# Attention read and soft mixture of experts in one kernel: twelve identity transposes ahead of the first load, and the first states moved from ACT's queue to SP's

## The chip, the cores and the metric

The kernel runs on one core of a Trainium2 chip. A core has five engines that each work through their own instructions in order: PE (TensorE, matrix products and transposes), DVE (VectorE), ACT (ScalarE), POOL (GpSimd) and SP (SyncE, which here only issues DMA transfers). PE loads its weights by separate instructions, shown as PEld. Transfers run on 16 DMA engines, whichever engine issued them. The metric is the device time of one execution in microseconds (us).

## The reference

Inputs: `x` of 8 batches, 8 heads, 512 tokens and 64 channels; `state` of 8 batches, 8 heads, 32 states and 64 channels; all f32.

```python
def _attn_ref(x, state):
    scores = scale * np.matmul(x, state.transpose(0, 1, 3, 2))
    a = softmax(scores)                     # over the 32 states
    xread = np.matmul(a, state)
    scores2 = scale * np.matmul(state, x.transpose(0, 1, 3, 2))
    a2 = softmax(scores2)                   # over the 512 tokens
    sread = np.matmul(a2, x)
    return np.concatenate([xread, sread], axis=2)

def _moe_ref(x, phi, w1, w2):               # x: 4608 rows (8 batches x 544) of 512
    logits = x @ phi                        # 32 slots = 8 experts x 4
    d = softmax over the rows of logits
    slot_input = d.T @ x
    for e in range(E):
        h = np.maximum(slot_input[e] @ w1[e], 0.0)
        slot_out[e] = h @ w2[e]
    c = softmax over the slots of logits
    return c @ slot_out
```

The softmaxes are written out in the reference with the maximum subtracted and 1e-9 added to the sum; `w1` is 8 x 512 x 1024, `w2` is 8 x 1024 x 512.

## The kernel before

The kernel has two stages. The first computes attention for batch 0 to 7 and gathers what the experts read. The second multiplies with `w1` (into `h_ps`), with `w2` (into `so_ps`), and writes the output.

The first stage is a list of small steps, `ORDER`, which is executed in the order in which it is written; each step issues a few instructions, and each engine then works through its own in that order. Steps that matter here, `b` the batch, `g` one of the four parts of a batch of `x` (two heads each), `h` one of two halves:

- `X.b.g` (PE, L203): four transposes of 128x128 of a part of `x` against the identity `ident`, into a PSUM buffer of the pool `ps_t`, which has three buffers that are used in turn.
- `xe.b.g` (ACT, L208): copies that buffer to SBUF as `xt` (times 0.125), which frees it.
- `S.b` (PE, L217): the scores `sc` of a batch, from its four `xt` and from its states `stT_sb`.
- `q`, `m1`, `m2` (DVE, L230, L235, L266): transposes the scores and takes maxima. `sub` (POOL, L239) subtracts, `x1` (ACT, L242) takes the exponential, `l1` (DVE, L246) sums.
- `G.0` (PE, L186) multiplies the states by `phi_bd`. `phi_bd` is a copy of the loaded `phi_sb` that POOL makes (L180). It is issued ahead of the whole list, so it stands before the first `sub` in POOL's order.

Batch 0 of `x` is loaded in four parts of 256 KB, 128 partitions by 512 elements, the others in two transfers of 512 KB. The states of batches 0 and 1 come as one transfer (128 KB, `stT_sb[:, 0:1]`, called the first states below), those of the other six as another (384 KB, the other states). In the kernel before, ACT issues the first states and then parts 1 and 3; SP issues parts 0 and 2, batch 1, the other states, `phi_sb`, batches 2 to 7, and then the weights. The transfers take eight semaphores in turn, and a transfer that reuses one waits on its issuing engine until the one eight places earlier has landed.

```python
    act.dma_start(stT_sb[:, 0:1], stT[:, 0:1])
...
            if b == 0:
                for g, eng in enumerate((nc.sync, act)):
                    eng.dma_start(t[:, g], xv[:, 2 * k + g])
            else:
                nc.sync.dma_start(t, xv[:, 2 * k : 2 * k + 2])
```

`ident` is made by POOL at the start (a memset and a select, masks.py). The buffers `big` hold `x`, states and weights; a weight is loaded when a buffer is free (`load_w`), in the second stage after each step of `w1_part` (L639) and `w2_part` (L699).

Of the kernel before, what the change touches and what calls it, by code (L numbers as in the profile page):

```python
# [8 lines left out]
F32 = mybir.dt.float32  # L9
# [6 lines left out]
P = 128  # L16
B = 8
S = 512
# [46 lines left out]
def attention_soft_moe(ctx: ExitStack, tc: tile.TileContext, x, stT, phi, w1, w2, out_x, out_s):  # L65
# [6 lines left out]
    nc = tc.nc  # L72
    pe, act, dve, pool = nc.tensor, nc.scalar, nc.vector, nc.gpsimd
# [5 lines left out]

    stT_sb = big.tile([P, 4, 2, 2, 2, NS], F32, tag="big", name="stT_sb")  # L80
    phi_sb = cp.tile([P, 4, NS], F32, name="phi_sb")
    act.dma_start(stT_sb[:, 0:1], stT[:, 0:1])
    xb = []
    for b in range(B):
        for k in range(2):
            t = big.tile([P, 2, NJ, 2 * D], F32, tag="big", name=f"x{b}_{k}")
            xv = x[b].rearrange("p (g j c) -> p g j c", g=4, j=NJ)
# [3 lines that stand above are left out]
            else:  # L91
                nc.sync.dma_start(t, xv[:, 2 * k : 2 * k + 2])
            xb.append(t)
        if b == 1:
            nc.sync.dma_start(stT_sb[:, 1:4], stT[:, 1:4])
            nc.sync.dma_start(phi_sb, phi)
# [29 lines left out]
    ident = cp.tile([P, P], F32, name="ident")  # L126
# [27 lines left out]
    with ExitStack() as actx:  # L154
# [3 lines left out]
        ps_t = actx.enter_context(tc.tile_pool(name="ps_t", bufs=3, space=PSUM))  # L158
# [13 lines left out]

        def mtile(shape, name):
            return ps_m.tile(shape, F32, tag="ms", name=name)


        phi_bd = wk.tile([P, 4, 2, NS], F32, tag="h", name="phi_bd", bufs=NH)
# [126 lines left out]
        def R_(b, h):  # L304
            r = R[b]
            if h == 0:
                r["srp"] = mtile([P, 2, D], f"sr_ps{b}")
            for j in range(NJ):
                for g in range(4):
                    pe.matmul(  # L310
                        r["srp"][32 * g : 32 * g + 32, h, :],
                        r[f"eT{h}"][:, j, 32 * g : 32 * g + 32],
                        xb[2 * b + g // 2][:, g % 2, j, D * h : D * h + D],
                        start=(j == 0),
                        stop=(j == NJ - 1),
                    )
            if h == 1:
                load_w(2)
# [6 lines left out]
        def srT(b):  # L325
            r = R[b]
            r["srTp"] = mtile([P, P], f"srT_ps{b}")
            pe.transpose(r["srTp"], r["sr"].rearrange("p h d -> p (h d)"), ident)
# [8 lines left out]
        def Lx(b, h):  # L337
            q, i = group(b)
            if h == 0 and i == 0:
                q["lt"] = mtile([P, len(q["b"]), P], f"lt_{b}")  # L340
            for j in range(NJ):
                pe.matmul(
                    q["lt"][32 * j : 32 * j + 32, i, :],
                    G_sb[:, b, h, :],
                    R[b][f"aT{h}"][:, P * j : P * j + P],
                    start=(h == 0),
                    stop=(h == 1),
                )
# [486 lines left out]
```

## Time and profile before

| | us |
|---|---|
| median of 3 runs | 137.98 (137.72 to 139.47) |
| profiled execution, its own time | 137.19 |
| span of the profiled execution, first to last instruction | 135.4 |
| PE busy | 115.8 (86% of the span) |
| DVE busy | 85.9 (63%) |
| ACT busy | 79.0 (58%) |
| POOL busy | 44.8 (33%) |
| DMA, mean rate | 382 GB/s, 51.76 MB |

The page cuts the span into 40 slices of 3.4 us and gives the busy share of each engine in tenths. In its groups, a row reads: line, engine, operation, output <- input, sizes, count. The timeline gives start, duration and count, and in brackets the idle time ahead and what ended it; SPq and ACTq are the DMA instructions on those engines' queues. Lists of transfers give the size and the time from issue to landing. The row of granted clock on the page stands at full speed from the start, so how fast PE runs is read from the durations of equal instructions.

### The profile page before, as it was taken

The page shows a single profiled execution, that of the slowest core. Times are in us where ns is not written, and L with a number is a line of the kernel's source. Part 1 is how long each engine was busy: PE and PEld are TensorE (multiplying, and loading weights), DVE is VectorE, ACT ScalarE, POOL GpSimd, SP SyncE. Part 2 cuts the span into 40 slices and gives each one's busy share as a digit, 9 for nine tenths or more (in the row PEclk, how much of TensorE's full clock was granted, in tenths as well). Part 3 has the DMA queues.
Part 4 walks back from the last instruction along what each step waited for, and adds up shares of the span by engine and source line. Part 5 has one row for each costly group of instructions (what it writes and reads, how often), then busy time and mean ns, then how long its engine had stood idle before and what let it go on. Part 6 is the DMA issues. An engine that isn't in the chain of part 4 may idle for free.

```text
span 135.4 us, 5043 instructions
## 1 busy us (share of the span) xinstructions
PE 115.8 (86%) x2103; PEld 81.8 (60%) x2103; DVE 85.9 (63%) x216; ACT 79.0 (58%) x195; POOL 44.8 (33%) x64
## 2 busy tenths in 40 slices
PE   0479899999999999999989968999997999999500
PEld 0354667869597875757766748962596458493100
DVE  2002999999999999999998359209930361524700
ACT  3042999999999998897994920410101371625600
POOL 3001635376375535338778163402500000000000
PEclk9999999999999999999999999999999999999955
DMA  3999999999999999999999952999999999999992
GB/s 86 307 408 421 421 414 420 413 418 420 415 410 421 412 422 413 419 414 424 412 413 418 416 236 62 407 415 418 419 420 412 422 404 413 413 413 377 420 416 92
DMA packets 14854, 51.76 MB, mean 382 GB/s; under 512 B 1648, under 2 KB 1904, under 8 KB 14832
## 3 DMA queue, kind: packets, MB, share of 16 engines
q1 hardware_dynamic: 14400, 50.80, 93.4%
q10 hardware_dynamic: 432, 0.66, 1.4%
q8 instruction: 16, 0.26, 0.7%
q14 instruction: 6, 0.05, 0.1%
HBM read 42.53 MB, written 8.91 MB: 380 GB/s over the span
## 4 chain that ended last, share of the span: by engine, by line
DVE 41%; PE 37%; ACT 7%; issue 4%; DMA 4%; DVEq 1%; ACTq 0%
PE so_ps L699 11%; PE h_ps L639 11%; DVE l1s L246 7%; PE o L729 7%; DVE aT L260 6%; DVE q L230 6%; DVE nm L266 6%; DVE m L235 5%; DMA x<-x_in 4%; DVE r L251 3%; ACT xt L208 2%; PE xt_ps L203 2%; PE sc L217 2%; PE os L747 2%; DVE r L250 1%
## 5 line engine op out<-in xcount | busy, mean ns | idle before, releaser
L203 PE MATMUL xt_ps<-ident,x 128*128 128x128 f32 x128 | 20.1, 296 | 6.1 <-DMA x<-x_in 5.3
L208 ACT ACTIVATE xt<-xt_ps 128x512 f32<-128x512 f32 x32 | 18.8, 617 | 7.6 <-PE xt_ps L203 7.6
L239 POOL TENSOR_TENSOR q<-q,m 128x512 f32<-128x512 f32 x16 | 16.7, 1049 | 19.0 <-DVE m L235 11.9
L739 DVE COPY out<-o 128x512 f32<-128x512 f32 x16 | 10.3, 686 | 18.6 <-PE o L729 18.6
L203 PEld LDWEIGHTS xt_ps<-ident,x 128*128 128x128 f32 x128 | 15.4, 151 | 9.6 <-issue 5.7
L255 POOL TENSOR_TENSOR q<-q,r 128x512 f32<-128x512 f32 x16 | 16.7, 1049 | 8.0 <-DVE r L251 2.7
L230 DVE STREAM_TRANSPOSE q<-sc 128x512 f32<-128x512 f32 x16 | 11.1, 695 | 10.3 <-PE sc L217 10.3
L699 PEld LDWEIGHTS so_ps<-w,h_m 128*32 128x32 f32 x512 | 13.8, 110 | 4.2 <-issue 4.1
L699 PE MATMUL so_ps<-w,h_m 128*32 128x128 f32 x512 | 15.6, 274 | 0.7 <-issue 0.7
L639 PE MATMUL h_ps<-w,si_m 128*32 128x512 f32 x128 | 14.4, 594 | 0.4 <-DVE si_m L611 0.4
L738 ACT COPY out<-o 128x512 f32<-128x512 f32 x16 | 8.6, 588 | 7.2 <-PE o L729 7.2
L271 ACT ACTIVATE e<-sc,nm 128x512 f32<-128x512 f32 x16 | 11.2, 706 | 1.2 <-DVE q L230 0.4
L639 PEld LDWEIGHTS h_ps<-w,si_m 128*32 128x32 f32 x128 | 9.1, 110 | 4.2 <-issue 2.9
L260 DVE STREAM_TRANSPOSE aT<-q 128x512 f32<-128x512 f32 x16 | 10.6, 684 | 0.0
L246 DVE TENSOR_REDUCE l1s<-q 128x16 f32<-128x512 f32 x16 | 10.5, 657 | 0.0
L310 PE MATMUL sr_ps<-x,eT 128*32 128x64 f32 x512 | 10.3, 220 | 0.3 <-ACT eT L293 0.3
L242 ACT ACTIVATE q<-q 128x512 f32<-128x512 f32 x16 | 10.5, 658 | 0.0
L266 DVE TENSOR_REDUCE nm<-sc 128x1 f32<-128x512 f32 x16 | 10.5, 660 | 0.0
L235 DVE TENSOR_REDUCE m<-q 128x16 f32<-128x512 f32 x16 | 10.5, 659 | 0.0
L285 PE MATMUL eT_ps<-ident,e 128*128 128x128 f32 x64 | 10.0, 279 | 0.5 <-ACT e L271 0.5
L217 PE MATMUL sc<-xt,stT_sb 64*32 64x512 f32 x128 | 10.2, 653 | 0.0
L285 PE MATMUL an_ps<-ident,aT 128*128 128x128 f32 x64 | 9.9, 280 | 0.2 <-DVE aT L260 0.2
(115 smaller groups left out, 179.5 us busy)
## 6 DMA issues: line engine op xcount, KB each, us to landing
w<-w_in SPq DMA_DIRECT2D x64, 512.0 KB, 10.0
out_x<-out SPq DMA_DIRECT2D x16, 512.0 KB, 6.4
x<-x_in SPq DMA_DIRECT2D x14, 512.0 KB, 8.3
x<-x_in SPq DMA_DIRECT2D x2, 256.0 KB, 4.0
x<-x_in ACTq DMA_DIRECT2D x2, 256.0 KB, 6.2
out_s<-out_s SPq DMA_DIRECT2D x2, 256.0 KB, 5.9
stT_sb<-stT_in SPq DMA_DIRECT2D x1, 384.0 KB, 8.2
stT_sb<-stT_in ACTq DMA_DIRECT2D x1, 128.0 KB, 3.7
```

The costliest lines, as they stand in the source:

```text
L203: pe.transpose(p[:, P * j : P * j + P], xb[2 * b + g // 2][:, g % 2, j, :], ident)
L208: act.mul(r[f"xt{g}"], r[f"xp{g}"], 0.125)
L230: dve.transpose(r[f"q{h}"], r[f"sp{h}"])
L235: dve.tensor_reduce(out=r[f"m1{h}"], in_=r[f"qv{h}"], axis=AX.X, op=ALU.max)
L239: pool.tensor_tensor(v, v, R[b][f"m1{h}"].broadcast_to([P, 16, NS]), op=ALU.subtract)
L246: dve.tensor_reduce(out=l1s[:, i, :, 0:1], in_=R[b][f"qv{h}"], axis=AX.X, op=ALU.add)
L255: pool.tensor_tensor(v, v, R[b][f"r1{h}"].broadcast_to([P, 16, NS]), op=ALU.mult)
L260: dve.transpose(r[f"aT{h}"], r[f"q{h}"])
L266: dve.tensor_reduce(out=r[f"nm2{h}"], in_=r[f"sp{h}"], axis=AX.X, op=ALU.max, negate=True)
L285: pe.transpose(p[:, j, :], r[f"{src}{h}"][:, P * j : P * j + P], ident)
L639: pe.matmul(h_ps[hf][32 * kt : 32 * kt + 32, :], si_m[kt // 2][:, 256 * (kt % 2) + 32 * e : 256 * (kt % 2) + 32 * e + 32], w1t[hf, e, kt], ...
L699: pe.matmul(so[k][32 * i : 32 * i + 32, :], h_m[hf][:, 256 * i + 32 * e : 256 * i + 32 * e + 32], w2t[k, e, 4 * hf + i], start=(hf == 0 an ...
```

## The change

The first states leave ACT's queue and are issued by SP behind parts 0 and 2 of batch 0. ACT issues parts 1 and 3 alone. PE gets twelve transposes of the identity against itself into a buffer `spin` of the pool `ps_t`, ahead of the first step; nothing reads them.

```diff
     stT_sb = big.tile([P, 4, 2, 2, 2, NS], F32, tag="big", name="stT_sb")
     phi_sb = cp.tile([P, 4, NS], F32, name="phi_sb")
-    act.dma_start(stT_sb[:, 0:1], stT[:, 0:1])
     xb = []
...
             xb.append(t)
+        if b == 0:
+            nc.sync.dma_start(stT_sb[:, 0:1], stT[:, 0:1])
         if b == 1:
             nc.sync.dma_start(stT_sb[:, 1:4], stT[:, 1:4])
             nc.sync.dma_start(phi_sb, phi)
...
             return ps_m.tile(shape, F32, tag="ms", name=name)
+
+
+        spin = ps_t.tile([P, S], F32, tag="tr", name="spin")
+        for i in range(12):
+            pe.transpose(spin[:, P * (i % 4) : P * (i % 4) + P], ident, ident)
```

The rows below are the first of each engine, in its own order; lines are those of the two kernels (L90, L92 before are L89, L91 after; L203 is L209; L217 is L223). Names carry a running number at their end; `x_0` is the tile of parts 0 and 1 of a batch, `x_1` that of parts 2 and 3. First ACT at the start of the program, before and then after:

```order
L82 DMA stT_sb<-stT_in 128x256
L90 DMA x_0_66<-x_in 128x512
L90 DMA x_1_69<-x_in 128x512
L208 ACT_TABLE_LOAD
L208 ACTIVATE xt_1_211<-xt_ps_1_201 128x512
```

```order
L89 DMA x_0_65<-x_in 128x512
L89 DMA x_1_68<-x_in 128x512
L214 ACT_TABLE_LOAD
L214 ACTIVATE xt_1_224<-xt_ps_1_214 128x512
L214 ACTIVATE xt_0_226<-xt_ps_0_209 128x512
```

Parts 1 and 3 each move up by one place. The copies behind them keep their order (part 1 before part 0). Now SP at the start, before and then after:

```order
L90 DMA x_0_66<-x_in 128x512
L90 DMA x_1_69<-x_in 128x512
L92 DMA x_0_72<-x_in 128x1024
L92 DMA x_1_74<-x_in 128x1024
L95 DMA stT_sb<-stT_in 128x768
L96 DMA phi_sb<-phi_in 128x128
L92 DMA x_0_78<-x_in 128x1024
```

```order
L89 DMA x_0_65<-x_in 128x512
L89 DMA x_1_68<-x_in 128x512
L94 DMA stT_sb<-stT_in 128x256
L91 DMA x_0_72<-x_in 128x1024
L91 DMA x_1_74<-x_in 128x1024
L96 DMA stT_sb<-stT_in 128x768
L97 DMA phi_sb<-phi_in 128x128
L91 DMA x_0_78<-x_in 128x1024
```

The first states stand third on SP; batch 1, the other states and `phi_sb` each move down by one. Before, `phi_sb` waited on SP for the first states to land; now it waits for part 1. Last PE at the start, after the change:

```order
L180 MATMUL spin<-ident 128x128 x12
L209 MATMUL xt_ps_0_209<-ident,x_0_65 128x128 x4
L209 MATMUL xt_ps_1_214<-ident,x_0_65 128x128 x4
L209 MATMUL xt_ps_2_219<-ident,x_1_68 128x128 x4
L209 MATMUL xt_ps_3_230<-ident,x_1_68 128x128 x4
L223 MATMUL sc_0_237<-xt_0_226,stT_sb 32x512
```

The twelve transposes are the only new rows on PE. `spin` takes the first buffer of `ps_t`, so each later tile of that pool sits one buffer further on; the fourth part's buffer still comes free with the copy of part 0, as before. DVE's and POOL's rows are as they were.

## The prediction, made before the changed kernel ran

> **What bounds the kernel now.** I read the stretches of time first. Columns: start:end, length, busy time and count of PE, PEld, DVE, ACT and POOL, granted clock, DMA share, GB/s.
>
> ```profile
> 20.00:40.00 20.00, 19.70 (x378) 15.59 (x379) 19.78 (x47) 19.68 (x48) 11.49 (x12) 1.00 1.03 416
> 40.00:60.00 20.00, 19.25 (x391) 14.09 (x389) 19.65 (x54) 18.92 (x51) 8.61 (x10) 1.00 1.03 417
> 79.00:85.00 6.00, 4.48 (x59) 3.89 (x55) 5.17 (x16) 0.62 (x1) 3.17 (x4) 1.00 0.37 122
> 85.00:95.00 10.00, 10.00 (x94) 6.13 (x89) 3.79 (x12) 1.59 (x4) 2.31 (x3) 1.00 1.03 417
> ```
>
> In the middle of the first stage DVE works 19.78 of 20 us, so this stage ends as much earlier as DVE's stream starts earlier, if nothing else holds it. The DMA engines run full (1.03) around one hole, 79 to 85 us, where the second stage has not yet freed buffers. Then the start, in the chain of waits (start, us, what):
>
> ```profile
> 1.17 5.13 DMA x<-x_in
> ...
> 6.34 1.13 PE xt_ps L203 x4
> ...
> 7.49 1.58 ACT xt L208 x3
> ...
> 9.12 1.09 PE xt_ps L203 x4
> 10.21 2.35 PE sc L217 x16
> ```
>
> DVE's first work on scores starts when `S.0` ends (12.55). Ahead of that stand a late part 1, the transposes, ACT's copies, the transposes of part 3, and 2.4 us of scores. Equal PE instructions are slower here than later (line, engine, operation, count, ns min/median/max, first and last start):
>
> ```profile
> L203 PE MATMUL xt_ps<-ident,x x12: 421/421/476, 4.3 to 7.9; 128*128 128x128 f32 x12
> L203 PE MATMUL xt_ps<-ident,x x16: 272/273/330, 12.5 to 14.2; 128*128 128x128 f32 x16
> L217 PE MATMUL sc<-xt,stT_sb x16: 801/1056/1060, 10.1 to 11.8; 64*32 64x512 f32 x16
> L217 PE MATMUL sc<-xt,stT_sb x16: 589/601/613, 17.2 to 17.8; 64*32 64x512 f32 x16
> ```
>
> PE runs at about 57% speed until the last scores of `S.0` (801 lies between 1056 and 601, so it changes near 12.3), and fast from then on.
>
> **The change, part by part.** All sums are made against the profiled execution: 137.19 us of its own, span 135.4, so 1.8 lie around the span. It is 0.8 under the median of 137.98.
>
> *The twelve transposes.* The identity's select, and PE's blocks in the timeline (start, us, ..., idle before and what ended it):
>
> ```profile
> 1.01 0.29 POOL masks.py:199 TENSOR_SCALAR_AFFINE_SELECT ident<-ident 128x128 f32<-128x128 f32 x1
> 6.34 1.97 PE L203 MATMUL xt_ps<-ident,x 128*128 128x128 f32 x8 [0.91 <-DMA x<-x_in]
> 12.48 2.00 PE L203 MATMUL xt_ps<-ident,x 128*128 128x128 f32 x16
> 17.19 1.18 PE L217 MATMUL sc<-xt,stT_sb 64*32 64x512 f32 x16
> ```
>
> At the early speed, transposes follow each other every (1.97 - 0.42)/7 = 0.22 us, at the later speed every (2.00 - 0.27)/15 = 0.115. Twelve from 1.35 at the early speed take 11 x 0.22 + 0.42 = 2.84 and end at 4.2, when part 0 lands (below): they cost nothing, being in idle time. What they may bring is an earlier fast PE. Before, 1.97 us of unbroken work (6.34 to 8.31) did not make it fast; the unbroken stretch from 9.12 to 12.3, 3.2 us, did. Work from 1.35 on, followed without a break over 0.2 us by slow parts 0 and 1, gives fast PE at 4.6 at the earliest. I take 6, and 8 as the late bound.
>
> The Trainium skill, page "TensorE: Matmul & The Clock Gate", part 1 ("The HAM clock gate"), says that activity is judged in windows of 3.4 us that run freely, not from the kernel's start. The 3.2 us above agree with a window; by that rule PE's full speed comes at 4.8 to 8.2, anywhere between from run to run, which my bounds already span. The same part calls the slow phase's penalty under 1% of a typical span: by that alone the time would not fall under 135.8. The rows of the chain speak against using it so, since here the slow stretch stands ahead of everything that DVE does.
>
> *The loads.* First issues, then size and time from issue to landing:
>
> ```profile
> 0.73 0.41 ACTq L82 DMA_DIRECT2D stT_sb<-stT_in  x1
> 0.74 0.85 SPq L90 DMA_DIRECT2D x<-x_in  x2
> 1.17 0.94 ACTq L90 DMA_DIRECT2D x<-x_in  x2
> ...
> stT_sb<-stT_in ACTq DMA_DIRECT2D x1, 128.0 KB, 3.7
> x<-x_in SPq DMA_DIRECT2D x1, 256.0 KB, 3.5
> x<-x_in SPq DMA_DIRECT2D x1, 256.0 KB, 4.5
> x<-x_in ACTq DMA_DIRECT2D x1, 256.0 KB, 5.1
> x<-x_in ACTq DMA_DIRECT2D x1, 256.0 KB, 7.3
> ```
>
> So part 0 lands at 4.24, the first states at 4.43, part 2 (issued at 1.16) at 5.7, part 1 at 6.3, part 3 (issued at 1.64) at 8.9. SP's batch 1, issued from 1.64 on, runs beside parts 1 and 3 and delays them. Counted by landings, 384 KB are there at 4.43 and 896 at 6.3. After the change parts 0 and 1 share the engines first: 512 KB at 4.43 + 1.87 x 128/512 = 4.9. At the same 0.47 us for each 128 KB, parts 2 and 3 make 1024 KB at 6.8, and the first states 1152 KB at 7.2. These are estimates from the landings above. Bounds for part 3: 5.7, where SP's second 256 KB landed, and 8.9, as now. I take 6.8.
>
> The same skill's page "DMA: Bandwidth & Descriptors" ("Issuing engines are not separate DMA queues") says that all issuers share the 16 engines and a second issuer saves only issue time. By that alone part 3 would land 0.4 us earlier, at 8.5, its transposes with it, which is rival 4 below. The trace has 7.3 us for 256 KB on ACT beside 4.5 on SP, issued half a microsecond apart, so which queue carries what did matter for landing.
>
> *`S.0` after the change.* Parts 0 and 1 are transposed by 6.0 (fast) to 6.9 (slow, 1.97 from 4.9). ACT then copies part 1 and part 0, some 0.55 each (1.58 for three): the buffer of part 3 is free at 7.1 to 8.0, later than the part lands. Its transposes take 0.66, its copy 0.6, and the last scores end some 0.7 after: 9.1 to 10.0. That is 2.55 to 3.45 earlier than 12.55; I take 3.0. The first states (7.2) are there before `S.0` begins.
>
> *What is late next.* The rows of POOL, ACT and DVE after `S.0`, and `phi_sb`:
>
> ```profile
> 4.42 0.33 SPq L96 DMA_DIRECT2D phi_sb<-phi_in  x1
> ...
> phi_sb<-phi_in SPq DMA_DIRECT2D x1, 64.0 KB, 6.5
> ...
> 11.08 0.62 POOL L180 COPY phi_bd<-phi_sb 64x128 f32<-64x128 f32 x2 [9.34 <-DMA phi_sb<-phi_in]
> 14.62 1.05 POOL L239 TENSOR_TENSOR q<-q,m 128x512 f32<-128x512 f32 x1 [2.93 <-DVE m L235]
> ...
> 15.76 0.66 ACT L242 ACTIVATE q<-q 128x512 f32<-128x512 f32 x1
> ...
> 16.45 0.69 DVE L246 TENSOR_REDUCE l1s<-q 128x16 f32<-128x512 f32 x1
> ```
>
> `phi_sb` lands at 10.92 and POOL copies until 11.70. `sub.0.0` stands behind these copies in POOL's order and has 2.9 us to spare now. The change does not bring `phi_sb` earlier: the bytes ahead of it on both queues are the same 2560 KB, and the 0.5 us later issue (it waits for part 1, 4.9, no longer for the states, 4.4) still finds SP's queue full. So `sub.0.0` starts at 11.72 at the earliest, `x1.0.0` at 12.86, and DVE's `l1.0.0` at 13.55: **2.9 us earlier and no more**, and all that DVE does later follows. This cap and the 3.0 of `S.0` lie close; with both of them I take 2.8 for the first stage (2.5 to 3.2; the upper end if `phi_sb` lands 0.3 earlier).
>
> *Does it reach the end?* Loads and outputs fill the DMA engines from 85 us to the end, so the second stage ends earlier only if they restart earlier. The hole of 79 to 85 us holds 6 x (1.03 - 0.37) = 4.0 us of transfers, more than 2.8. But single engines lag (here the columns are length, granted clock, DMA share, GB/s):
>
> ```profile
> 81.50:82.00 0.50, 1.00 0.08 33
> 82.00:82.50 0.50, 1.00 0.00 0
> ...
> 83.00:83.50 0.50, 1.00 0.00 0
> 83.50:84.00 0.50, 1.00 0.71 90
> ...
> 131.50:132.00 0.50, 0.50 1.03 422
> ...
> 133.00:133.50 0.50, 0.50 0.18 74
> ```
>
> A few engines still move the last weights until 82.0, and the second stage's first transfers start at 83.5. Restarting 2.8 earlier, at 80.7, they find the slowest still busy for 1.3 us. At the end of the kernel, too, the engines run full until 132 and the slowest until nearly 134. If these are not the same engines, a lag of 1.3 ends within those 2 us and costs nothing, which I take. If they are, only the 1.5 us of 82.0 to 83.5 are won.
>
> **Sum:** 0 (twelve transposes) - 2.8 (first stage) + 0 (hole) = -2.8; 137.19 - 2.8 = **134.4**.
>
> **The rivals.**
>
> 1. *A DMA engine that lags in both places takes part of the gain.* Only 1.5 us (2.0 at most, with the lag before 82) reach the end: 135.7, or 135.2. For it: full DMA engines from 85 us on. Against: nothing shows the engine to be the same.
> 2. *The clock does not come up with the twelve transposes.* Identity work may count for little, or a pause at 4.2 may reset it. Then parts 0 to 2 end at 7.9 and the scores follow slowly: from the start of part 3's transposes to the end of `S.0` it took 12.55 - 9.12 = 3.43, so 8.0 + 3.43 = 11.4, 1.1 earlier: 136.1. Against it: PE would have worked for over 6 us. The skill's bound of 1% on the slow phase, cited above, would end near here too, at 135.8 or more.
> 3. *`phi_sb` is no cap.* If it lands early, the early bound of `S.0` counts, 3.45: 133.7.
> 4. *Part 3 gains only ACT's earlier issue.* It lands at 8.97 - 0.44 = 8.5 (1.17 to 0.73 in the issues). With PE fast by then, transposes of 0.66, a copy of 0.6 and 0.7 for the last scores end `S.0` at 10.4 to 10.5, 2.1 earlier: 135.1. This is the same as what the skill's rule on issuers would give. Against it: SP's own 256 KB landed in 4.5.
> 5. *Slower: the first states come late on SP's queue.* They gate all of `S.0`. With PE fast it decides from a landing at 12.55 - 1.18 = 11.4. If they took 11.4 us from their issue at 1.6, as the slowest transfer of `x` did:
>
> ```profile
> DMA to landing us min/median/max: 3.5/7.7/11.4
> ```
>
> they would land at 13.0 and `S.0` would end at 14.2, 1.65 later: 138.8. Against it: SP's third transfer of now, four times as large, landed 6.8 us after issue.
>
> ```profile
> x<-x_in SPq DMA_DIRECT2D x1, 512.0 KB, 6.8
> ```
>
> **How the numbers follow.** Forecast 0.55, rival 1 0.15, rival 2 0.12, rival 3 0.08, rival 4 0.07, rival 5 0.03. The range 133.5 to 135.8 covers the forecast with its bounds (2.5 to 3.2, so 134.0 to 134.7) and rivals 1, 3 and 4, and leaves out 2 and 5. Two per cent, about what a measurement of this kernel tells from no change, is 135.2 from the median: under it lie the forecast, rival 3, rival 4 and a little of rival 1, 0.71. Within 2% lie the rest of rival 1, rival 2 and most of rival 5: 0.28. Slower by over 2%: 0.01.
>
> **What would show it.** In the profile after: twelve transposes from 1.35 to about 4.2; scores of `S.0` near 600 ns, ending at 9.1 to 10.0; part 3 landing near 6.8; POOL idle until `phi_sb` at about 11, then `sub.0.0` right behind its copies; `l1.0.0` at 13.5 instead of 16.45; the first products with `w1` 2.8 earlier than now; the DMA hole shrunk to about 1 us. I am wrong if the scores of `S.0` still take 1056 ns, if `l1.0.0` comes far from 13.5, or if the first stage ends 2.8 earlier and the kernel does not.

## The result, and the profile after

The changed kernel takes 134.2 us (median of 4 executions, 134.10 to 136.28) against 137.85 before (median of 4, 137.31 to 139.47). The ratio is 0.9746 with a 95% interval of 0.9707 to 0.9784: 2.5% faster. The profiled execution took 134.10 us, its span is 132.3. Executions more than 1.5% above the fastest of the same kernel (136.28 and 139.47 here) are left out of the ratio.

First the timeline of the changed kernel at its start: start, us, engine, line, operation, count, and the idle time ahead with what ended it.

```profile
1.36 2.82 PE L180 MATMUL spin<-ident 128*128 128x128 f32 x12 [1.36 <-POOL ident masks.py:199]
4.66 2.17 PE L209 MATMUL xt_ps<-ident,x 128*128 128x128 f32 x12 [0.48 <-DMA x<-x_in]
6.43 2.06 ACT L214 ACTIVATE xt<-xt_ps 128x512 f32<-128x512 f32 x4 [3.49 <-PE xt_ps L209]
7.08 0.66 PE L209 MATMUL xt_ps<-ident,x 128*128 128x128 f32 x4 [0.25 <-ACT xt L214]
7.66 1.93 PE L223 MATMUL sc<-xt,stT_sb 64*32 64x512 f32 x16
9.62 0.72 DVE L236 STREAM_TRANSPOSE q<-sc 128x512 f32<-128x512 f32 x1 [7.33 <-PE sc L223]
11.20 0.61 POOL L186 COPY phi_bd<-phi_sb 64x128 f32<-64x128 f32 x2 [9.46 <-DMA phi_sb<-phi_in]
11.90 2.08 POOL L245 TENSOR_TENSOR q<-q,m 128x512 f32<-128x512 f32 x2
12.97 0.63 ACT L248 ACTIVATE q<-q 128x512 f32<-128x512 f32 x1
13.64 0.69 DVE L252 TENSOR_REDUCE l1s<-q 128x16 f32<-128x512 f32 x1 [0.19 <-ACT q L248]
```

The added transposes end at 4.18. Part 3's four transposes start at 7.08 instead of 9.12. `S.0` ends at 9.59 instead of 12.55, and DVE's `l1.0.0` starts at 13.64 instead of 16.45. The chain of waits, which led through part 1 of `x` and then PE and ACT before, leads through `phi_sb` in this profile:

```profile
0.73 4.05 DMA x<-x_in
...
4.80 6.26 DMA phi_sb<-phi_in
...
11.20 0.29 POOL phi_bd L186
...
11.53 0.30 POOL phi_bd L186
...
11.90 1.06 POOL q L245
...
12.97 0.64 ACT q L248
...
13.64 0.70 DVE l1s L252
```

Durations in the changed kernel (ns min/median/max, first and last start), then the loads of batch 0 by size and time to landing:

```profile
L180 PE MATMUL spin<-ident x12: 421/421/475, 1.4 to 3.8; 128*128 128x128 f32 x12
...
L223 PE MATMUL sc<-xt,stT_sb x16: 589/601/613, 7.7 to 9.0; 64*32 64x512 f32 x16
...
x<-x_in ACTq DMA_DIRECT2D x1, 256.0 KB, 4.0
x<-x_in SPq DMA_DIRECT2D x1, 256.0 KB, 3.9
...
x<-x_in ACTq DMA_DIRECT2D x1, 256.0 KB, 5.3
x<-x_in SPq DMA_DIRECT2D x1, 256.0 KB, 4.8
stT_sb<-stT_in SPq DMA_DIRECT2D x1, 128.0 KB, 5.7
```

All scores of `S.0` now take some 600 ns (a median of 1056 before). Part 3 lands 5.3 us after its issue (7.3 before), the first states 5.7 after theirs (3.7 before, but now not late for anybody). Last the start of the second stage, and the DMA engines in the hole and at the end (length, granted clock, DMA share, GB/s):

```profile
78.97 9.06 PE L645 MATMUL h_ps<-w,si_m 128*32 128x512 f32 x80 [0.35 <-DVE si_m L617]
80.14 4.03 SPq L107 DMA_DIRECT2D w<-w_in  x8
...
76.00:82.00 6.00, 1.00 0.83 302
82.00:92.00 10.00, 1.00 1.01 403
...
130.50:131.00 0.50, 0.50 0.18 74
131.00:131.50 0.50, 0.50 0.00 0
```

The products with `w1` start 2.67 us earlier, and the hole has shrunk from 6 x (1.03 - 0.37) = 4.0 us of transfers to 6 x (1.01 - 0.83) = 1.1.

### The profile page after: what moved, and what is told of

It reads as the page before. It is cut to its first block, busy times and chain, and to the rows that moved or that the text cites. A ratio compares the mean times of both kernels' runs of the same rounds, so it can differ in the third digit from the quotient of the medians.

```text
span 132.3 us, 5069 instructions
## 1 busy us (share of the span) xinstructions
PE 117.1 (89%) x2115; PEld 84.1 (64%) x2115; DVE 86.0 (65%) x216; ACT 79.0 (60%) x195; POOL 44.8 (34%) x64
## 4 chain that ended last, share of the span: by engine, by line
DVE 41%; PE 34%; DMA 8%; ACT 5%; issue 5%; POOL 1%; DVEq 1%; ACTq 0%; POOLq 0%
PE so_ps L705 11%; PE h_ps L645 11%; DVE l1s L252 7%; PE o L735 7%; DVE aT L266 7%; DVE q L236 6%; DVE nm L272 5%; DVE m L241 5%; DMA phi_sb<-phi_in 5%; DMA x<-x_in 3%; DVE r L257 3%; PE os L753 2%; DVE r L256 1%; ACT out L744 1%; DVE sr L329 1%
## 5 line engine op out<-in xcount | busy, mean ns | idle before, releaser
L209 PE MATMUL xt_ps<-ident,x 128*128 128x128 f32 x128 | 18.8, 284 | 0.7 <-DMA x<-x_in 0.5
L209 PEld LDWEIGHTS xt_ps<-ident,x 128*128 128x128 f32 x128 | 14.8, 146 | 3.7 <-DMA x<-x_in 1.7
L316 PEld LDWEIGHTS sr_ps<-x,eT 128*32 128x32 f32 x512 | 8.6, 110 | 2.5 <-ACT lt_all L358 0.8
```

The source lines that it names most:

```text
L209: pe.transpose(p[:, P * j : P * j + P], xb[2 * b + g // 2][:, g % 2, j, :], ident)
L316: pe.matmul(r["srp"][32 * g : 32 * g + 32, h, :], r[f"eT{h}"][:, j, 32 * g : 32 * g + 32], xb[2 * b + g // 2][:, g % 2, j, D * h : D * h + D],
```

## The experiments

Times are medians of all executions; each group of runs ran on one chip beside the kernel before. Single times of one kernel spread over 1 to 2 us, so where less than that matters I read the steps' start in the profiles. Those vary too: the second stage of the changed kernel starts at 78.97 in two profiles and at 79.99 in a third.

**The changed kernel again.** Its neighbours are the next three runs.

> The changed kernel again, as the neighbour of the three next runs: 134.2 us. S.0 ends near 9.6 us, phi_sb lands near 11.1, l1.0.0 starts near 13.6.

Measured: 134.78 us, ratio 0.9757 (0.9684 to 0.9831). `l1.0.0` starts at 13.59, the first products with `w1` at 78.97. Here the chain of waits leads to `l1.0.0` through PE and the copies on ACT, which end at 12.92 as `x1.0.0` starts, and not through `phi_sb`.

**`phi_sb` early.**

```diff
         if b == 0:
             nc.sync.dma_start(stT_sb[:, 0:1], stT[:, 0:1])
+            act.dma_start(phi_sb, phi)
         if b == 1:
             nc.sync.dma_start(stT_sb[:, 1:4], stT[:, 1:4])
-            nc.sync.dma_start(phi_sb, phi)
```

> The changed kernel with phi_sb issued by ACT behind parts 1 and 3, so that it lands by 8 us and POOL's copies are done long before sub.0.0. Theory A (the late phi_sb is the cap, through POOL): the cap and the end of S.0 lie 0.15 us apart, so l1.0.0 moves from 13.64 to 13.5 and the time falls by 0.15, to 134.05. Theory B (the cap is ACT: x1.0.0 stands behind the copies of batch 1, which follow S.0 and the landing of batch 1's second half at 9.9): nothing moves, 134.2.

Measured: 135.53 us, ratio 0.9818 (0.9737 to 0.9899). Its timeline:

```profile
7.61 0.61 POOL L186 COPY phi_bd<-phi_sb 64x128 f32<-64x128 f32 x2 [5.88 <-DMA phi_sb<-phi_in]
...
11.31 1.05 POOL L245 TENSOR_TENSOR q<-q,m 128x512 f32<-128x512 f32 x1 [3.09 <-DVE m L241]
...
11.94 1.08 ACT L214 ACTIVATE xt<-xt_ps 128x512 f32<-128x512 f32 x2
...
12.89 0.65 ACT L248 ACTIVATE q<-q 128x512 f32<-128x512 f32 x1
...
13.58 0.69 DVE L252 TENSOR_REDUCE l1s<-q 128x16 f32<-128x512 f32 x1 [0.47 <-ACT q L248]
```

`phi_bd` is ready at 8.2 and `sub.0.0` starts 0.6 earlier, ending at 12.36. Yet `x1.0.0` starts at 12.89, behind two copies of batch 1 on ACT, and `l1.0.0` at 13.58. Taking the cap of `phi_sb` away wins 0.06 us there: ACT's order holds the same place.

The median is 0.75 above the changed kernel's beside it. In this profile PE pauses for 0.72 us at 18.5, in the middle of one group of products (`sr_ps`), for no wait that the profile shows; DVE waits 0.70 us for them, and the second stage starts at 79.57. The third profile of the changed kernel has the same pause (0.77 us, stage at 79.99), so the moved `phi_sb` need not be its cause, which stays open.

**`phi_sb` early, and two of the four copies on DVE.** The edit beside the one above:

```diff
-            act.mul(r[f"xt{g}"], r[f"xp{g}"], 0.125)
+            if b == 0 and g in (0, 3):
+                dve.tensor_scalar_mul(r[f"xt{g}"], r[f"xp{g}"], 0.125)
+            else:
+                act.mul(r[f"xt{g}"], r[f"xp{g}"], 0.125)
```

> As the run with phi_sb early, and in batch 0 DVE copies parts 0 and 3 while ACT copies parts 1 and 2, so that S.0 ends near 8.8 instead of 9.6. Theory A: nothing else holds DVE, sub.0.0 starts near 10.8, l1.0.0 near 12.6, and the time falls by 1.0, to 133.2. Theory B: ACT's copies of batch 1 still wait for its second half (9.9), x1.0.0 stays near 12.8, l1.0.0 near 13.45, and the time falls by 0.2, to 134.0.

Measured: 134.81 us, ratio 0.9764 (0.9660 to 0.9869). `S.0` did not end at 8.8 but at 9.3: PE waits for a load until 6.40, and the scores start at 7.39, right behind the landing of the first states. So the test is weaker than planned. `l1.0.0` starts at 13.63, as theory B has it.

**The same with `x1.0.0` ahead of one copy on ACT.**

```diff
-X.1.0 E.0.0 xe.1.3 m1.0.0 G.0 q.0.1 sub.0.0 m1.0.1 xe.1.0 m2.0.1 x1.0.0 l1.0.0
+X.1.0 E.0.0 xe.1.3 m1.0.0 G.0 q.0.1 sub.0.0 m1.0.1 x1.0.0 xe.1.0 m2.0.1 l1.0.0
```

> As the run before, and x1.0.0 issued ahead of the copy of batch 1's part 0 on ACT. Theory A: as the run before, 133.2. Theory B: x1.0.0 gains the 0.55 us of one copy, l1.0.0 starts near 12.9, and the time falls to 133.5, 0.5 below the run before.

Measured: 134.69 us, ratio 0.9742 (0.9666 to 0.9819). Its timeline:

```profile
12.39 0.63 ACT L251 ACTIVATE q<-q 128x512 f32<-128x512 f32 x1
...
13.05 0.69 DVE L255 TENSOR_REDUCE l1s<-q 128x16 f32<-128x512 f32 x1
...
78.89 9.06 PE L648 MATMUL h_ps<-w,si_m 128*32 128x512 f32 x80 [0.35 <-DVE si_m L620]
```

With ACT's order changed, `l1.0.0` does start earlier, by 0.58 against the run before. That settles what held it. But the second stage starts at 78.89 (79.09 in the run before, 78.97 in the changed kernel): the half microsecond is lost on the way, and the time shows no gain. More than half goes at once. The copy that `x1.0.0` passed now stands ahead of `x1.0.1` on ACT, which starts at 14.07 instead of 14.13, and DVE's `l1.0.1` starts at 14.72 instead of 14.97. Later DVE waits for PE: its first transpose of scores after 27 us starts at 27.80 (27.89 in the changed kernel), and the chain of waits behind it is PE's work alone from 20 us on.

**The transposes alone,** the loads issued as before.

> The twelve transposes alone, the loads issued as before. Theory (both parts are needed, since S.0 waits for the last of loads, PE speed and copies): part 3 still lands near 8.9, its transposes and the scores run at full speed, S.0 ends near 10.9 instead of 12.55, 1.6 us are won: 135.6. Rival, PE's speed alone is the gain: 134.2. Rival, the loads alone: 137.2.

Measured: 137.38 us, ratio 0.9935 (0.9883 to 0.9987). Not the 1.6 us expected; no execution came down to 135.6. In its profile PE does not come to full speed in time:

```profile
1.36 2.82 PE L179 MATMUL spin<-ident 128*128 128x128 f32 x12 [1.36 <-POOL ident masks.py:199]
4.67 1.12 PE L208 MATMUL xt_ps<-ident,x 128*128 128x128 f32 x4 [0.49 <-DMA x<-x_in]
6.50 1.97 PE L208 MATMUL xt_ps<-ident,x 128*128 128x128 f32 x8 [0.71 <-DMA x<-x_in]
9.14 1.09 PE L208 MATMUL xt_ps<-ident,x 128*128 128x128 f32 x4 [0.66 <-DMA x<-x_in]
...
L222 PE MATMUL sc<-xt,stT_sb x16: 1057/1057/1061, 10.2 to 11.8; 64*32 64x512 f32 x16
```

Part 1 and part 3 are as late as before, PE pauses three times for loads, and all 16 products of `S.0` take 1057 ns. In this profile the transposes of the identity did nothing for them. It is one profile, of an execution of 138.21 us; the ten went from 136.01 to 140.03, which leaves room for some in which they did a little.

**The moved loads alone,** without the transposes.

> The moved loads alone, without the twelve transposes. Theory: parts land as in the changed kernel (part 3 near 6.4), PE works slowly without a break from 4.66 and becomes fast between 8 and 11, S.0 ends at 10.3 to 11.3, 1.25 to 2.25 us are won: 135.0 to 136.0, and 135.5 as the middle. Rival, PE's speed alone is the gain: 137.2. Rival, the loads alone: 134.2.

Measured: 135.17 us, ratio 0.9786 (0.9712 to 0.9860). In its profile DVE starts on the scores at 9.99 (9.62 in the changed kernel), `l1.0.0` starts at 13.86, and the second stage at 79.03. `S.0` ends at 9.96, earlier than expected, because PE came to full speed at 7.64 by the trace's record of its clock.

**`phi_sb` late.** In the changed kernel the transfer is issued behind batch 2 (`if b == 2`) instead of behind batch 1.

> The changed kernel with phi_sb issued behind batch 2 instead of ahead of it, so that it lands near 13.6 instead of 11.06. Theory A (POOL copies phi_sb ahead of sub.0.0): the copies end near 14.4, sub.0.0, x1.0.0 and l1.0.0 follow at 14.5, 15.6 and 16.3, 2.6 us later than in the changed kernel: 136.8. Rival (phi_sb is not on the path): 134.2.

Measured: 137.14 us, ratio 0.9960 (0.9923 to 0.9997). Its timeline:

```profile
13.69 0.61 POOL L187 COPY phi_bd<-phi_sb 64x128 f32<-64x128 f32 x2 [11.95 <-DMA phi_sb<-phi_in]
...
14.39 2.06 POOL L246 TENSOR_TENSOR q<-q,m 128x512 f32<-128x512 f32 x2
15.47 0.63 ACT L249 ACTIVATE q<-q 128x512 f32<-128x512 f32 x1 [2.51 <-POOL q L246]
16.13 0.69 DVE L253 TENSOR_REDUCE l1s<-q 128x16 f32<-128x512 f32 x1 [2.69 <-ACT q L249]
```

DVE stands idle for 2.69 us, `l1.0.0` starts 2.5 later, the second stage 2.3 later (81.29), and nearly the whole gain is gone. So the path from `phi_sb` through POOL is real, and a delay on it goes on into the second stage.

**Two copies on DVE alone,** `phi_sb` as in the changed kernel.

> The changed kernel with the copies of parts 0 and 3 of batch 0 on DVE, phi_sb as in the changed kernel. S.0 ends near 8.8 instead of 9.6. Theory A (cap by phi_sb): sub.0.0 stays at 11.9, l1.0.0 at 13.6, 134.2. Rival (S.0 alone sets DVE's start): 0.8 less, 133.4.

Measured: 134.49 us, ratio 0.9729 (0.9651 to 0.9807). `S.0` ends at 9.2, 0.4 earlier and not 0.8. `l1.0.0` starts at 13.54, 0.1 earlier. The 0.8 us of the rival did not come.

**Four kernels side by side,** with and without the twelve transposes, and with and without eight more on PE ahead of the second stage, where PE is idle. The eight:

```diff
-Y.3 Yf SI SIe
+Y.3 Yf FZ SI SIe
...
+        def FZ():
+            t = ps_t.tile([P, S], F32, tag="tr", name="fill")
+            for i in range(8):
+                pe.transpose(t[:, P * (i % 4) : P * (i % 4) + P], ident, ident)
```

> The changed kernel once more, as the neighbour of the next three: 134.2 to 134.8 us in the middle, single runs up to 136.3. Where PE's granted clock is 0.50 for 3.4 us near 80 us, the products with w1 take 1.7 us longer and so does the kernel.

> The moved loads without the twelve transposes. Theory C (the loads alone are the gain, since PE then works without a break from part 0 on and becomes fast by itself): within 0.3 us of its neighbour with the transposes. Rival (the transposes are worth the 0.3 to 0.4 us by which S.0 ends earlier, and more when PE becomes fast late): 0.4 to 1.0 us slower than that neighbour.

> The changed kernel with eight more transposes of the identity on PE in its idle time between the last px and si (77.1 to 78.3 us), which nothing reads. Theory D (PE's clock is halved for 3.4 us in those executions in which a window of that length holds too little PE work, near the start of the second stage): the clock stays at 1.00 there in the profile, 80 products with w1 take 9.06 us, single runs no longer reach above 135, and the middle falls by 0 to 0.8 us. Rival (the halved clock has nothing to do with that idle time): nothing changes, or the eight transposes delay si and cost 0.1.

> The moved loads and the eight transposes near 78 us, without the twelve at the start. Theory C: within 0.3 us of the run with both. Rival to it: 0.4 to 1.0 us slower than that run. With the second stage's clock kept up in both, this pair is the sharper of the two comparisons.

| | us | range of its executions | ratio |
|---|---|---|---|
| changed kernel | 134.81 | 134.21 to 136.67 | 0.9769 (0.9717 to 0.9821) |
| moved loads alone | 135.21 | 134.47 to 135.98 | 0.9815 (0.9761 to 0.9869) |
| changed, with the eight | 134.60 | 134.21 to 135.07 | 0.9769 (0.9723 to 0.9815) |
| moved loads, with the eight | 135.06 | 134.52 to 135.68 | 0.9804 (0.9755 to 0.9853) |

The twelve transposes are worth 0.40 and 0.46 us by the medians of the two pairs, 0.6 and 0.5 by the ratios, with intervals that overlap. So the rival to theory C is nearer, by times that do not settle it. The profiles say why it can be so. Without the transposes, PE comes to full speed at another moment in each. In the second of these four runs it comes too late for `S.0`:

```profile
L218 PE MATMUL sc<-xt,stT_sb x16: 945/1058/1059, 8.4 to 10.0; 64*32 64x512 f32 x16
...
10.99 0.72 DVE L231 STREAM_TRANSPOSE q<-sc 128x512 f32<-128x512 f32 x1 [8.71 <-PE sc L218]
```

In the three profiles with the moved loads alone (the last with the eight transposes), DVE's first transpose of scores starts at 9.99, 10.99 and 10.39. In the nine with both parts of the change, some with further edits, it starts at 9.19 to 9.62. In the three `l1.0.0` follows 3.87 us later each time, at 13.86, 14.86 and 14.26, and the second stage starts at 79.03, 80.02 and 79.63: there the end of `S.0` sets the start, and what it loses goes on.

The trace's record of the clock gives the moment: 7.64, 10.72 and 9.58 us in the three, 4.80 to 6.59 in the nine, 12.17 before the change, 13.25 with the transposes alone. In all fourteen profiles PE is busy for at least 2.83 us of the 3.41 us just before that moment, and for at most 2.67 us of each earlier stretch of 3.41 us, counted back from it. With the transposes alone, the stretches from 3.01 and from 6.42 hold 2.29 and 2.67 us, with the pauses for loads in them.

The eight transposes run from 77.05 to 78.14 and delay nothing: `si`, PE's last step ahead of the second stage, starts at 78.29, the products with `w1` at 78.94 (78.97 in two profiles of the changed kernel). The median is 0.2 us lower, which is no difference by these runs. The last section says what they were for. No kernel here is clearly better than the changed one.

## Why the prediction was right

134.4 was forecast, 134.2 measured, and 134.78 and 134.81 in two repeats. By its steps:

- **The transposes in idle time.** Forecast to end at 4.2, they end at 4.18. The pause behind them is longer than thought (0.48 us, not under 0.2), because part 0 lands at 4.6 instead of 4.24. The moved loads need not be the reason: with the transposes alone it is 0.49.
- **Fast PE.** Put at 6, with 4.6 and 8 as bounds. By the record of the clock it came at 6.01, and at 4.80 to 6.59 in the nine profiles. The forecast went by the length of unbroken work (3.2 us). The profiles go by PE's share of a stretch of 3.41 us, which may hold pauses.
- **The loads.** Part 1 was put at 4.9 and landed at 4.7, part 3 at 6.8 and 6.5, the first states at 7.2 and 7.3. The Trainium skill ("DMA: Bandwidth & Descriptors", "Issuing engines are not separate DMA queues") has a second issuer save only issue time. The runs differ: moving 128 KB from one queue to the other brought part 3's landing from 8.9 to 6.5.
- **`S.0`.** Forecast 9.1 to 10.0, it ends at 9.59.
- **The cap.** `phi_sb` lands at 11.06 (forecast 10.92) and `l1.0.0` starts at 13.64 (13.55). The number held, but the step named POOL alone, while ACT's order holds `x1.0.0` to 12.9 as well, which the runs with `phi_sb` early and with `x1.0.0` moved show. The two limits lie within 0.1 us of each other; that the second lay no later was luck.
- **"All that DVE does later follows".** True of a delay (`phi_sb` late: 2.5 and then 2.3). Not true of a gain beyond the changed kernel's: 0.58 at `l1.0.0` became 0.2 at the second stage, behind ACT's order and then PE. And a pause of PE on the way can cost 0.7.
- **The hole.** The second stage starts 2.67 earlier (forecast 2.8), and the span is 3.1 shorter. The lagging DMA engine of rival 1 took nothing. At the end the last transfers are done by 131.0, where before they took until 134.0. So the end won 0.4 more than the start of the stage. The repeat of the changed kernel starts the stage at 78.97 too, but its last transfers take until 131.5 and its span is 132.9, 0.6 longer: the extra lies in how the last transfers run out, and that varies by itself.

What the prediction did not say is how the gain divides. It treated the two parts of the change as one sum. Moving the loads is most of it (2.1% and 1.9% alone, 2.3 to 2.5% with both). It brings part 3 earlier, and it also lets PE work on without pauses, so that PE comes to full speed by itself. The transposes alone are worth 0.65% by the ratio (0.1 to 1.2%). Beside the move they made that moment early in all nine profiles. Rival 2 put the time at 136.1 if the transposes did not bring the clock up. That price was too high: without them the moved loads took 135.2, PE coming to full speed by itself at 7.64 to 10.72.

## What to carry to other kernels

When a start waits for several loads, count when the last one lands for each order of issue: a small transfer in the short queue ahead of two needed ones can cost more than its own bytes. Work that keeps PE busy paid here only where it joined up with the real work behind it. Behind a wait that is taken away, look for all that ends within a tenth of a microsecond of the next one, by the order of every engine on the path.

## What the runs showed that was not expected

PE's clock is halved once more in some executions, at the start of the second stage, for 3.4 us. It shows in six of the twelve profiles of the experiments, and in neither of the two profiles of before and after. Here are three stretches of the run with two copies on DVE (length, PE busy, clock, DMA share, GB/s) and its products with `w1`:

```profile
76.50:79.90 3.40, 1.88 (x31) 1.00 0.91 369
79.90:83.30 3.40, 3.40 (x21) 0.50 0.66 229
83.30:86.70 3.40, 3.40 (x37) 1.00 1.03 408
...
79.07 10.76 PE L648 MATMUL h_ps<-w,si_m 128*32 128x512 f32 x80 [0.35 <-DVE si_m L620]
```

The same stretches of the changed kernel, with the same PE work in the first:

```profile
76.50:79.90 3.40, 1.88 (x28) 1.00 0.92 375
79.90:83.30 3.40, 3.40 (x37) 1.00 0.77 246
```

Both kernels start the stage within 0.1 us of each other (79.07, 78.97), but 80 products take 10.76 us instead of 9.06, and the execution 135.44 instead of 134.10. So the same pause of PE halves the clock in one execution and not in the other. The Trainium skill ("TensorE: Matmul & The Clock Gate", "The HAM clock gate") has activity judged in windows of 3.4 us that run freely: the length of the halved stretch agrees, and a window's place would explain the chance. The same page of the Trainium skill has the clock fall after an idle window; here PE was busy for 1.88 us of the 3.4 just before.

The traces bear the windows out. In each profile the changes of the clock on record lie a whole number of 3.413 us apart, and the halved stretch is one of these. Laid out from these changes, the window that ends where the clock falls holds 1.89 or 1.90 us of PE's work in all six profiles that show it. In the changed kernel the same pause is split between two windows, with 2.78 and 2.44 us, and the clock stays up. It stays up in every profile in which no window there holds less than 2.03 us. One profile speaks against a clean limit: the run with `x1.0.0` moved has a window with 1.89 us too (76.90 to 80.31) and keeps its clock.

The eight transposes fill that pause. In both of their profiles the 80 products take 9.06 us, and no execution of the changed kernel with them was above 135.07 (136.67 without). The window around the pause then holds 2.91 or 2.92 us of PE's work, far from the 1.89 at which the clock fell. Two profiles and six executions are still too few to call this shown.
